# Chunked attention with a gated MLP on one core: the transfers of V to the two partition halves alternate, and the first three units load V in eight pieces

## The chip, the cores and the metric

The program runs on one core of one Trainium2 chip. The metric is the time of one execution on the device in microseconds, lower is better. The inputs are laid out on the host before the launch (q and k transposed, V rolled and cut into chunks of 32 rows), and that is not part of the time.

## The reference

Everything is float32. The attention part has batch B = 4, heads H = 8, length S = 768 and head size D = 64. Each chunk of 32 queries sees 8 memory keys and a window of 16 keys to the left, its own 32, and 8 to the right.

```python
for c in range(nc):                              # 24 chunks of 32 queries
    k_full = concatenate([mem_k, k[l_start:r_end]])
    v_full = concatenate([mem_v, v[l_start:r_end]])
    scores = scale * q_c @ k_full.T
    a = exp(scores - max(scores)); a = a / (sum(a) + 1e-9)
    out[:, :, chunk] = a @ v_full
x = out as (4, 768, 512)
h = relu(x @ w_in)                               # 512 -> 1024
u, v = h[..., :512], h[..., 512:]
v_n = (v - mean(v)) / sqrt(var(v) + 1e-6)
v_s = w_spatial @ v_n + b_spatial                # mixes the 768 tokens
return (u * v_s) @ w_out                         # 512 -> 512
```

## The kernel before

**Units.** The attention is cut into 24 units of 128 tokens (4 chunks, all 8 heads); six units make one batch. Each unit i goes through the same steps: ACT copies its keys into `kmain` (L375), PE makes the scores `sx<-kmain,q` (L388, "S" below), VectorE subtracts the maximum (`mx` L441, `p` L445), ACT takes the exponential (L450), VectorE sums (L455 to L458), PE transposes the weights (`pt`, L472), ACT copies them to `pT` (L475), PE multiplies them by V (`sx<-vmain,pT`, L388, "A" below), VectorE scales the result (`xs`, L424), PE transposes it (`xt`, L487), and the result is split into a high part (`x`, ACT L492) and a low part (`x`, VectorE L496). `p` and `pT` have one buffer each.

**MLP.** Each product by `w_in` is three matmuls per 128 columns: high by high (L525), low by high (L526) and high by low (L527). `ffn_v` makes one group per unit (128x512), `ffn_u` four per three units (128x384). The weights come as float64 in eight transfers `big<-in_moe_w_in_dram`; ACT (L825, L830), VectorE (L834, L835) and GpSimd (L840) turn each into float32, and L854 and L858 split it into `win_h` and `win_l`. The normalized v half and the u half go out to DRAM (`vn_far`, `u_far`) and come back for the second part, in which the spatial product and `w_out` are done with Strassen-like sums (L647 to L686).

**V in SBUF.** `vmain` holds three units. Partitions 0 to 63 serve the even heads (r = 0), 64 to 127 the odd heads (r = 1). In each half the first 32 rows are the chunk's own, 8 rows hold the memory values (written by the spread copies, L370), and 24 rows come from the next chunk. So a unit's V takes four transfers, of 32, 24, 32 and 24 partitions with runs of 1 KB, 0.46 MB together. `load_v` issues them, and `v_keys` names what the product A of a unit has to wait for.

**What sets the order.** Nothing is written in execution order. `Plan` gets every operation with an engine, an estimated duration and a rank, simulates the engines and one DMA pipe (0.30 MB per us), and emits each engine's instructions in the order of that simulation. A transfer counts there with `slow` (for its size) times `drag`. Nearly all transfers are issued by SP, in the order of the plan; those of one `line` (q, k, V, weights) keep the order of the code, and the stores find places between them. Each engine executes strictly in its emitted order. SP's transfers share eight semaphores in turn (`DMAHW0` to `DMAHW7`), so a transfer is issued only after the one eight before it has landed. Beside that `held_by` paces them by megabytes, with a wide window for the first 9 MB.

```python
    load_qk(0, (0,)); load_qk(0, (1,))
    # four w_in_part(c, 1, ...), the columns of ffn_v
    load_v(0); load_qk(1); w_in_part(0, 0, ...)
    load_v(1); w_in_part(1, 0, ...)
    load_v(2); w_in_part(2, 0, ...); w_in_part(3, 0, ...)
    # from unit 1 on, attend(i) is followed by load_v(i + 2)
```

## Time and profile before

| what | value |
|---|---|
| three runs | 380.58, 380.65, 384.18 us; median 380.65 us |
| the profiled execution | 378.39 us, of which the span of the trace is 376.2 us |
| PE busy | 355.6 us, 95% |
| VectorE, ACT, GpSimd busy | 275.0 us (73%), 188.8 us (50%), 139.8 us (37%) |
| mean granted PE clock | 0.991 |
| DMA | 65.12 MB, mean 173 GB/s |

The share of each engine is an average over a start of some 40 us, a long middle and an end. The profiled execution lies 2.26 us below the median of the three runs, so a difference is best worked out against the profiled execution and then carried over to the median.

### The profile page before, as it was taken

Reading aid. Unit: us, or ns where it says so; the run is one execution under the profiler, and the core shown is the slowest. Engines: PE = TensorE matmul, PEld = TensorE weight load, DVE = VectorE, ACT = ScalarE, POOL = GpSimd, SP = SyncE. Lnnn points to the kernel's source line nnn. Section 1 sums busy time; section 2 is a strip of 40 time slices with the busy share of each in tenths; the row PEclk is TensorE's granted clock in tenths of the full one; section 3 lists DMA queues with packets and bytes.
Section 4 is the critical chain, followed back from the end, with each engine's and each line's share of the span. In section 5 each row is a group of like instructions: output and inputs, shape, how many; then the busy total and the mean of one; then the engine's idle time right before and its main releaser. Section 6 shows DMA issues by size and latency. Waiting matters only on the chain.

```text
span 376.2 us, 11734 instructions
## 1 busy us (share of the span) xinstructions
PE 355.6 (95%) x4964; PEld 327.8 (87%) x4964; DVE 275.0 (73%) x470; ACT 188.8 (50%) x336; POOL 139.8 (37%) x143
## 2 busy tenths in 40 slices
PE   1569899999999999999999999999999999999996
PEld 1357698898988988989889899999999999999996
DVE  3887875757767667775498589787858795896694
ACT  3757544554654456354473366327533742553371
POOL 5444652383484088510033195251026002203410
PEclk9969999999999999999999999999999999999999
DMA  8998888888786783865832649204720582140014
GB/s 230 290 233 228 186 250 232 230 234 250 218 237 192 251 232 92 264 212 181 233 142 92 216 142 319 101 0 167 250 89 0 170 257 80 61 144 8 2 44 167
DMA packets 47368, 65.12 MB, mean 173 GB/s; under 512 B 4434, under 2 KB 38866, under 8 KB 47316
## 3 DMA queue, kind: packets, MB, share of 16 engines
q1 hardware_dynamic: 46900, 64.25, 56.4%
q8 instruction: 39, 0.64, 0.7%
q10 hardware_dynamic: 416, 0.13, 0.1%
q14 instruction: 13, 0.11, 0.1%
HBM read 45.49 MB, written 18.87 MB: 171 GB/s over the span
## 4 chain that ended last, share of the span: by engine, by line
PE 91%; DVE 4%; ACT 2%; DMA 1%; issue 1%; SPq 0%; ACTq 0%; DVEq 0%
PE y L686 22%; PE f L686 17%; PE f L525 13%; PE f L526 12%; PE f L527 12%; PE sx L388 10%; PE xt L487 3%; PE pt L472 3%; DMA k<-in_k_dram 1%; DVE st L835 1%; DVE st L834 1%; DVE mx L441 1%; DVE p L445 0%; PE y L680 0%; PE f L680 0%
## 5 line engine op out<-in xcount | busy, mean ns | idle before, releaser
L742 POOL TENSOR_TENSOR ug<-st,ug 128x384 f32<-128x384 f32 x24 | 33.1, 1392 | 97.7 <-DVE st L734 97.7
L686 PE MATMUL y<-wsp,op 128*128 128x384 f32 x288 | 52.6, 336 | 0.0
L686 PEld LDWEIGHTS y<-wsp,op 128*128 128x128 f32 x288 | 50.1, 188 | 0.0
L525 PE MATMUL f<-x,win_h 128*128 128x384 f32 x128 | 46.3, 362 | 0.0
L527 PE MATMUL f<-x,win_h 128*128 128x384 f32 x128 | 43.1, 337 | 0.0
L526 PE MATMUL f<-x,win_l 128*128 128x384 f32 x128 | 43.0, 336 | 0.0
L525 PE MATMUL f<-win_h,x 128*128 128x512 f32 x96 | 41.7, 435 | 0.0
L686 PE MATMUL f<-wsp,op 128*128 128x384 f32 x216 | 40.1, 336 | 0.0
L526 PE MATMUL f<-win_h,x 128*128 128x512 f32 x96 | 38.6, 402 | 1.5 <-DVE x L496 1.5
L664 DVE TENSOR_TENSOR op<-sm,op 128x768 fp32r<-128x768 f32 x32 | 33.4, 1050 | 7.2 <-ACT op L661 6.6
L527 PE MATMUL f<-win_l,x 128*128 128x512 f32 x96 | 38.4, 400 | 0.0
L686 PEld LDWEIGHTS f<-wsp,op 128*128 128x128 f32 x216 | 37.6, 188 | 0.0
L686 PE MATMUL y<-wout,op 128*128 128x256 f32 x288 | 35.7, 280 | 0.0
L424 DVE TENSOR_TENSOR xs<-sx,rec 128x512 f32<-128x512 f32 x24 | 16.5, 689 | 25.8 <-PE sx L388 25.6
L686 PEld LDWEIGHTS y<-wout,op 128*128 128x128 f32 x288 | 34.8, 188 | 0.1
L661 ACT CAST op<-sm 128x768 fp32r<-128x768 f32 x32 | 26.3, 838 | 15.5 <-DVE sm L647 7.7
L571 POOL TENSOR_TENSOR rstd<-ve,mhalf 128x1 f32<-128x1 f32 x24 | 14.6, 610 | 52.2 <-DVE ve L567 51.8
L388 PEld LDWEIGHTS sx<-kmain,q 64*32 64x32 f32 x1536 | 17.5, 110 | 17.1 <-POOL vmain L370 9.5
L388 PE MATMUL sx<-kmain,q 64*32 64x64 f32 x1536 | 21.5, 235 | 10.6 <-ACT kmain L375 8.4
L596 ACT ACTIVATE uo<-f 128x384 f32<-128x384 f32 x32 | 15.6, 491 | 24.5 <-PE f L527 23.0
L370 POOL COPY vmain<-memv 8x1024 f32<-8x1024 f32 x22 | 23.5, 1075 | 10.2 <-PE sx L388 8.5
L686 PE MATMUL f<-wout,op 128*128 128x256 f32 x216 | 27.1, 280 | 0.0
(92 smaller groups left out, 732.8 us busy)
## 6 DMA issues: line engine op xcount, KB each, us to landing
vmain<-in_v_dram SPq DMA_DIRECT2D x48, 128.0 KB
vn_far<-st SPq DMA_DIRECT2D x24, 256.0 KB
u_far<-uo SPq DMA_DIRECT2D x32, 192.0 KB
vr<-vn_far SPq DMA_DIRECT2D x8, 768.0 KB
ug<-u_far SPq DMA_DIRECT2D x16, 384.0 KB
q<-in_q_dram SPq DMA_DIRECT2D x11, 512.0 KB
out_dram<-ot SPq DMA_DIRECT2D x36, 128.0 KB
vmain<-in_v_dram SPq DMA_DIRECT2D x47, 96.0 KB
```

The costliest lines, as they stand in the source:

```text
L370: {"DVE": nc.vector, "POOL": nc.gpsimd}[eng].tensor_copy(to, of)
L388: nc.tensor.matmul(o, w_, m, start=True, stop=True, skip_group_check=True)
L424: nc.vector.tensor_tensor(xs.rearrange("p t r d -> p r t d"), t_["sx", i][:, :, 1], rec.rearrange("p t r -> p r t").unsqueeze(3).broadcast ...
L525: nc.tensor.matmul(o, lh, rh, start=(j == 0), stop=False)
L526: nc.tensor.matmul(o, ll, rh, start=False, stop=False)
L527: nc.tensor.matmul(o, lh, rl, start=False, stop=(j == len(pairs) - 1))
L571: nc.gpsimd.tensor_tensor(a, t_["ve", i], mhalf, op=ALU.pow)
L596: op("ACT", act(HT), lambda: nc.scalar.activation(alloc("uo", i, [P, HT], F32), t_["f", n], AF.Relu), r=[("f", n)], w=[("uo", i)], rank=rank)
L661: nc.scalar.copy(half(0), of())
L664: nc.vector.tensor_tensor(half(1), of(), half(0).bitcast(F32), op=ALU.subtract)
L686: nc.tensor.matmul(o, x, y, start=first and m == 1 and not (seed and bank != "x"), stop=m == 3 * chunks, skip_group_check=True)
L742: nc.gpsimd.tensor_tensor(g, t_[st(x)], g, op=ALU.mult)
```

## The change

The transfers of one unit are issued in another order: first the 32-row transfer of each half, then the 24-row one of each half. For units 0, 1 and 2 each of them is cut in two along t (the pairs of heads), so that such a unit comes in eight transfers of 64 KB or 48 KB. The argument `second`, which no call used, goes. The plan's `drag` for V falls from 1.5 to 1.2, so the plan believes that V arrives sooner.

```diff
-    def load_v(i, seq=True, second="SP"):
+    def load_v(i, seq=True):
...
-        for r in range(2):
-            v4 = v_of(i).rearrange("p t c d -> p t (c d)")
...
-                load(dst, src_, w=[("vm", i, r, s)], rank=10.0 * i, slow=1.2, us=0.38, seq=seq, drag=1.5,
-                     eng=second if r else "SP")
-            part(v4[p0:p0 + CH], src(v, g0 * D, [[G * D, CH], [TS, T], [1, n * D]]), 0, CH)
-            o = v4[p0 + SLOT:p0 + D]
-            if g0 + 2 * (T - 1) * NC + n < G:
-                part(o, src(v, (g0 + 1) * D, [[G * D, nr], [TS, T], [1, n * D]]), 1, nr)
...
+        def part(r, dst, src_, s):
+            load(dst, src_, w=[("vm", i, r, s)], rank=10.0 * i, slow=1.2, us=0.38, seq=seq, drag=1.2)
+        v4 = v_of(i).rearrange("p t c d -> p t (c d)")
+        step = (T if i >= 3 else T // 2)
+        for t0 in range(0, T, step):
+            t1 = t0 + step
+            for r in range(2):
+                g0 = (b * H + r) * NC + c0
+                part(r, v4[r * D:r * D + CH, t0:t1], src(v, g0 * D + t0 * TS, [[G * D, CH], [TS, step], [1, n * D]]), t0)
+        for t0 in range(0, T, step):
+            t1 = t0 + step
+            for r in range(2):
+                g0 = (b * H + r) * NC + c0
+                o = v4[r * D + SLOT:r * D + D]
+                if g0 + 2 * (T - 1) * NC + n < G or t1 < T:
+                    part(r, o[:, t0:t1], src(v, (g0 + 1) * D + t0 * TS, [[G * D, nr], [TS, step], [1, n * D]]), T + t0)
...
     def v_keys(i):
-        return [("vm", i, r, s) for r in range(2) for s in range(4)] + \
+        return [("vm", i, r, s) for r in range(2) for s in range(2 * T + 2)] + \
```

The transfers of V are 110 instead of 98. Line numbers behind `load_v` are 7 higher in the changed kernel. Since the plan decides the order, the change also moves instructions that it does not name. Three places matter below.

On SP, at the start, behind the first four loads of `w_in`, before the change (`vmain` is V in SBUF, `big` the raw `w_in`):

```order
L257 DMA big<-in_moe_w_in_dram 128x1024 x4
L257 DMA vmain<-in_v_dram 32x4x256
L257 DMA vmain<-in_v_dram 24x4x256
L257 DMA vmain<-in_v_dram 32x4x256
L257 DMA vmain<-in_v_dram 24x4x256
L257 DMA q<-in_q_dram 128x4x256
L257 DMA k<-in_k_dram 128x4x288
L257 DMA big<-in_moe_w_in_dram 128x1024
```

and with the change:

```order
L257 DMA big<-in_moe_w_in_dram 128x1024 x4
L257 DMA vmain<-in_v_dram 32x2x256 x4
L257 DMA vmain<-in_v_dram 24x2x256 x4
L257 DMA q<-in_q_dram 128x4x256
L257 DMA k<-in_k_dram 128x4x288
L257 DMA big<-in_moe_w_in_dram 128x1024
```

The q and k of units 2 and 3 stand behind eight transfers instead of four.

On PE, at the start, around the first product by V (`sx<-vmain,pT`), before the change:

```order
L540 MATMUL f<-win_h 128x512 x4
L472 MATMUL pt<-ident,p 128x128 x4
L388 MATMUL sx<-vmain,pT 32x64 x32
L487 MATMUL xt<-ident,xs 128x128 x4
L388 MATMUL sx<-kmain_144,q 32x64 x32
```

and with the change:

```order
L547 MATMUL f<-win_h 128x512 x4
L395 MATMUL sx<-vmain,pT 32x64 x32
L479 MATMUL pt<-ident,p 128x128 x4
L494 MATMUL xt<-ident,xs 128x128 x4
L395 MATMUL sx<-kmain_144,q 32x64 x32
```

The product of unit 0 by V now stands ahead of the transpose of unit 1's weights.

On VectorE, in the third MLP group, around the low part of unit 2 (`x<-xt,x`), before the change:

```order
L424 TENSOR_TENSOR xs<-sx,rec 128x2x4x64
L441 TENSOR_REDUCE mx<-sx 128x8
L575 TENSOR_SCALAR st<-st,mvar,rstd 128x512
L834 TENSOR_SCALAR st<-st 128x512
L835 SCALAR_TENSOR_TENSOR st<-big,st 128x512
L445 TENSOR_TENSOR p<-sx,mx 128x2x4x64
L496 TENSOR_TENSOR x<-xt,x 128x4x128
L563 BN_STATS stats<-st 128x6
```

and with the change:

```order
L431 TENSOR_TENSOR xs<-sx,rec 128x2x4x64
L448 TENSOR_REDUCE mx<-sx 128x8
L452 TENSOR_TENSOR p<-sx,mx 128x2x4x64
L503 TENSOR_TENSOR x<-xt,x 128x4x128
L582 TENSOR_SCALAR st<-st,mvar,rstd 128x512
L841 TENSOR_SCALAR st<-st 128x512
L842 SCALAR_TENSOR_TENSOR st<-big,st 128x512
L570 BN_STATS stats<-st 128x6
```

The normalization of unit 0 and the two steps on `w_in` now stand behind the low part of unit 2 instead of ahead of it.

## The prediction

> **What bounds the kernel now.** I read the page first, then the busy time by stretches, then PE's waits.

> ```profile
> span 376.2 us, 11734 instructions
> PE 355.6 (95%) x4964; PEld 327.8 (87%) x4964; DVE 275.0 (73%) x470; ACT 188.8 (50%) x336; POOL 139.8 (37%) x143
> ```

> PE leaves only 376.2 - 355.6 = 20.6 us idle. In the stretches the columns are the length, the busy time of PE, PEld, DVE, ACT and POOL with their counts, the granted PE clock, the DMA share and GB/s.

> ```profile
> 0.00:10.00 10.00, 1.17 (x64) 0.96 (x64) 3.75 (x8) 2.94 (x4) 6.10 (x13) 1.00 0.85 240
> 10.00:20.00 10.00, 6.31 (x140) 4.36 (x140) 9.00 (x15) 7.54 (x14) 4.38 (x4) 1.00 1.10 288
> 20.00:25.00 5.00, 2.19 (x69) 1.79 (x70) 4.58 (x10) 3.66 (x7) 1.61 (x1) 0.74 0.96 227
> 25.00:30.00 5.00, 5.00 (x48) 3.68 (x47) 3.07 (x7) 1.58 (x4) 1.29 (x1) 0.58 0.97 249
> 30.00:35.00 5.00, 4.49 (x187) 3.55 (x172) 4.18 (x9) 4.21 (x8) 3.15 (x3) 1.00 0.96 244
> 35.00:40.00 5.00, 3.49 (x17) 2.43 (x17) 4.93 (x8) 3.98 (x7) 2.72 (x4) 1.00 0.66 199
> ...
> 42.00:200.00 158.00, 157.97 (x3244) 139.04 (x3230) 110.17 (x227) 82.62 (x145) 71.14 (x81) 1.00 0.71 211
> 200.00:364.00 164.00, 164.00 (x1135) 161.78 (x1134) 126.83 (x175) 77.65 (x141) 47.76 (x37) 1.00 0.36 122
> 364.00:376.20 12.20, 8.97 (x76) 8.72 (x75) 6.61 (x13) 3.98 (x10) 0.00 (x0) 1.00 0.38 130
> ```

> From 42 to 364 us PE is busy without a gap, so nothing can be won there, only lost. The last 12.2 us have 3.2 idle and hold no V. All the rest, 8.83 + 3.69 + 2.81 + 0 + 0.51 + 1.51 = 17.35 us, lies before 40 us. Who ends these waits:

> ```profile
> PE sx L388 <- ACT kmain L375: 8.4, 2, 7.1
> PE f L540 <- ACT win_h L854: 2.9, 1, 2.9
> PE xt L487 <- DVE xs L424: 1.9, 1, 1.9
> PE f L526 <- DVE x L496: 1.5, 1, 1.5
> ```

> These 14.7 of the 17.35 us wait for ACT and VectorE, none for a transfer of V. The 7.1 and the 2.9 come ahead of the first use of V. So a faster V by itself buys nothing; what can change the time is the order that the plan makes of it, and a V, q or k that comes too late.

> **Part 1: the transfers.** V moves slowly. Between 41 and 44 us SP's traffic is V alone; from 48 to 50 us it is mostly q and k, in runs of about the same size.

> ```profile
> 41.00:44.00 3.00, 3.00 (x75) 2.33 (x74) 2.83 (x6) 0.57 (x2) 2.76 (x3) 1.00 1.04 162
> 48.00:50.00 2.00, 2.00 (x73) 1.66 (x72) 1.22 (x2) 0.63 (x1) 1.94 (x3) 1.00 1.07 378
> ```

> A unit (0.46 MB) takes 2.8 us at 162 GB/s and would take 1.2 us at 378. Taking turns could win anything from 0 to 1.6 us of DMA time per unit; I take the lower quarter, 0.4, since each transfer still goes to one half only. On the sum it is worth 0 either way: DMA ended no wait of PE above, and its share is 0.71 in the long middle.

> [...] The rows here show the slow V, but nothing on alternation.

> **Part 2: eight pieces on SP.** Twelve more issues, and a transfer waits for the landing of the one eight before it.

> ```profile
> 10.75 0.39 SPq L257 DMA_DIRECT2D k<-in_k_dram  x1
> 14.43 0.35 SPq L257 DMA_DIRECT2D big<-in_moe_w_in_dram  x1
> 14.82 2.33 SPq L257 DMA_DIRECT2D vmain<-in_v_dram  x4
> 17.37 0.97 SPq L257 DMA_DIRECT2D big<-in_moe_w_in_dram  x1
> 19.10 5.04 SPq L257 DMA_DIRECT2D vmain<-in_v_dram  x4
> 24.79 0.82 SPq L257 DMA_DIRECT2D big<-in_moe_w_in_dram  x2
> ```

> One issue costs at most 2.33 / 4 = 0.58 us, waits included, the twelve 7.0 us of SP, spread over a start in which SP also waits (5.04 us for four). Now the eighth piece of unit 0 waits for the fourth `w_in` load. That one had landed by 14.82, when the transfer eight behind it went out. So the eighth piece leaves at about 14.8, q at 15.3, k at 15.9 instead of 10.75. That looks bad but is covered: unit 0's seven pieces keep the pipe full until then. From 14.8 on at most 0.46 MB of V at 162 GB/s (2.8 us) and 0.52 + 0.59 MB of q and k (128x4x256 and 128x4x288 floats) at 378 (2.9 us) are ahead, so k lands at 14.8 + 2.8 + 2.9 = 20.5, and V of unit 0 at 17.6. Who waits for them:

> ```profile
> 17.62 1.11 PE L472 MATMUL pt<-ident,p 128*128 128x128 f32 x4 [0.17 <-ACT p L450]
> 18.66 0.98 PE L388 MATMUL sx<-vmain,pT 64*32 64x64 f32 x64
> 19.76 0.59 ACT L475 COPY pT<-pt 128x512 f32<-128x512 f32 x1 [1.69 <-PE sx L388]
> 20.78 0.68 DVE L424 TENSOR_TENSOR xs<-sx,rec 128x512 f32<-128x512 f32 x1
> 22.21 0.59 ACT L492 CAST x<-xt 128x512 fp32r<-128x512 f32 x1 [1.34 <-PE xt L487]
> 22.69 0.73 ACT L375 COPY kmain<-k 128x640 f32<-128x640 f32 x1
> ```

> k is needed at 22.7, 2.2 us after my 20.5. V is needed by the A product, which the change puts ahead of pt: A at 17.7 to 18.7, pt to 19.8, the pT copy at 19.9 instead of 19.76. xs cannot start before 20.78 anyway, for VectorE is 4.58 of 5 us busy there, and ACT has 1.34 us to spare ahead of x. So V may land 1.34 - 0.14 = 1.2 us later, at 18.8, without cost. The first MLP group starts where it did. Term: 0, with bounds -0.2 and +0.5 us.

> **Part 3: the order on VectorE.** This is the one wait that the change takes up: PE's 1.51 us that end at 39.33. The first rows are of the chain, the last of ACT in order of time.

> ```profile
> 35.47 0.45 DVE st L575
> 35.92 1.45 DVE st L834
> 37.39 0.69 DVE st L835
> 38.08 0.60 DVE p L445
> 38.68 0.61 DVE x L496
> 39.33 0.50 PE f L526
> ...
> 36.70 0.57 ACT L492 CAST x<-xt 128x512 fp32r<-128x512 f32 x1
> ```

> The low part of unit 2 (`x`, L496) has its input from ACT at 36.70 + 0.57 = 37.27, but VectorE first normalizes unit 0 and works on `w_in` for 37.39 + 0.69 - 35.47 = 2.6 us. With the change p stands directly behind mx (35.47 to 36.1), and x follows when ACT is done: 37.3 + 0.7 = 38.0, so L526 starts near 38.06 instead of 39.33. **Gain 1.27 us**, at most the 1.51 that PE waited, and at least 0.7 if ACT, whose order changes there too (a step on `w_in` moves ahead of the cast to `win_h`), is late by one operation of 0.59. What is late next: the displaced L575, L834 and L835 now end near 39.7 instead of 38.1. L575 releases the store of unit 0, off the path. L834 and L835 feed GpSimd and `win_l` of a later column block, whose first reader is a `ffn_u` group; the plan fills that place with five blocks of other groups. Cost 0, or the 1.6 us of the displacement if that cover is gone.

> **Part 4: the rest of the order.** PE's 841 rows hold the same work, but up to unit 13 attention and MLP are interleaved otherwise. The tightest step is A, xs, xt: counting the matmuls between A and xt of a unit at 0.24 us (128x512) and 0.18 (128x384), the least before is 1.23 us, with the change 1.08 (unit 4) and twice 1.24 (units 5 and 8). xs takes 0.69, and with the semaphores some 0.9, so each fits, unless VectorE is on another 0.7 us operation when A ends; then the three places lose 0.5 + 0.35 + 0.35 = 1.2 us. I take 0.2, near the lower end, since in the whole of 42 to 200 us comparable places left PE idle for 0.03 us.

> **The sum** against the profiled execution: 0 + 0 - 1.27 + 0.2 = -1.1 us, 378.39 becomes 377.3 (span 375.1). That execution stands 2.26 us below the median of the runs shown, so the median goes from 380.65 to **379.5**, which I round to 379.4. This is a change of 0.3%, and about 1% is what a measurement of this kernel can tell from no change.

> **Rivals.**
> - *Given back.* The gain of part 3 is lost where the order is tighter (1.2 us of part 4) or where `win_l` comes late (1.6): the median stays at 380.7, at worst 382.1. For it: VectorE is busy 4.18 and 4.93 of 5 us from 30 to 40 us. Against: no gap of PE after 42 us.
> - *The clock.* PE was granted 0.74 and 0.58 from 20 to 30 us, and a matmul took twice as long:

> ```profile
> 26.23 0.43 PE f L525
> 41.20 0.24 PE f L525
> ```

>   If the changed start keeps PE busier, twelve matmuls gain 0.19 each, 2.3 us: 377.1 with part 3. Against: A moves ahead of pt, so the idle stretch before xt at 21.5 remains.
> - *Slower: the eighth piece.* Between 14.43 and 24.79, when the seventh `w_in` load goes out, SP issued ten transfers (1 + 4 + 1 + 4) with eight in flight, 8 x 1.04 = 8.3 us from issue to landing each. If the last piece of unit 0 takes that long, V lands at 23.1, and everything behind A (pt, pT, x, the keys of unit 2) moves with it. It decides from 18.8; the price is 4.3 us, and with part 3 the median is 383.7, or 385.0 when the gain of part 3 goes too. Against: those 8.3 us are the backlog of up to eight large transfers, and here only 0.46 MB is ahead.
> - *The change does not do what it says:* V stays at 162 GB/s because each transfer still goes to one half. Part 3 comes from the plan's lower `drag`, not from the chip, so the time is the forecast's, whose sum takes nothing from a faster V. I count it in the forecast.

> **How the numbers follow.** Forecast, with either rate of V, 0.58; given back 0.20; the clock 0.08; the eighth piece 0.08; an unforeseen start 0.06. The forecast's own sum runs from -1.51 - 0.2 = -1.7 to -0.7 + 0.5 + 0.2 = 0.0 us, a median of 378.9 to 380.7. To leave out no more than 2 in 10 the range reaches from the clock (377.1) nearly to the eighth piece: 376.8 to 382.8. Faster by over 1% (below 376.84) needs the clock and more of the start: 0.09. Slower by over 1% (above 384.46) needs the eighth piece with all else lost: 0.08. Within 1%: 0.83.

> **What would show it.** Right: PE's wait for `x` (L503 with its new number) falls from 1.5 us to 0.3 or less, the row of waits for `kmain`, `win_h` and `xs` stays within 0.3 us, PE is busy without a gap from 42 us on, and the first MLP matmul starts at 24.6 within 0.5. Part 1 is seen in GB/s where V is alone on SP: 162 now, some 185 by my 0.4 us. Part 2 is wrong if A of unit 0 waits for a transfer beyond 18.8 us or the keys of unit 2 come after 22.7. Part 4 is wrong if PE waits for `xs` or for the next `win_l` between 42 and 110 us. The whole is wrong if the granted clock of 20 to 30 us changes, or if a wait for k appears on ACT that holds up its evacuations of the MLP groups.

## The result and the profile after

The change takes **383.72 us** in the median of 20 runs (379.89 to 386.86), the kernel before 380.74 us (379.1 to 386.05) beside it. The ratio is 1.0074, 95% interval 1.005 to 1.0097: slower by 0.7%, where 379.4 us (0.3% faster) had been forecast. Run again in a second series it was 385.03 us against 382.23, ratio 1.0091 (1.0054 to 1.0128). Ratios here use the runs within 1.5% of the shortest of their kernel, which matters where a kernel's runs spread widely. The profile shown is of that second series, a run of 386.48 us; the one that came with the first (386.86 us) stops at the same places. Both stand near the top of their spread, and before's profile (378.39 us) is shorter than any of the 20 runs beside it. So the two profiles lie 8 us apart where the medians lie 3 us apart: the profiles show where time goes, not how much of it a median run loses.

The page of the change:

```profile
span 384.5 us, 11754 instructions
PE 357.6 (93%) x4964; PEld 329.4 (86%) x4964; DVE 275.0 (72%) x470; ACT 188.6 (49%) x336; POOL 139.7 (36%) x143
```

Against before's 376.2 and 355.6 the span is 8.3 us longer: PE is busy 2.0 us more for the same 4964 matmuls, and idle 26.9 instead of 20.6 us. PE's waits (total, times, longest):

```profile
PE sx L395 <- ACT kmain L382: 8.2, 2, 6.9
PE sx L395 <- issue: 6.3, 3, 4.3
PE f L547 <- ACT win_h L861: 2.9, 1, 2.9
PE xt L494 <- DVE xs L431: 2.6, 2, 2.3
...
PE f L533 <- issue: 1.6, 1, 1.6
```

The wait for `x` (1.5) is gone, as forecast, and those for `kmain` and `win_h` stand. New are 6.3 + 1.6 us of "issue": PE waits, and the profile names nothing that it waits for. Before had 0.3 us of it. The longest piece, in the rows of PE in order of time, first before, then the change:

```profile
32.69 0.78 PE L388 MATMUL sx<-vmain,pT 64*32 64x64 f32 x54
33.75 0.33 PE L388 MATMUL sx<-vmain,pT 64*32 64x64 f32 x10 [0.28 <-issue]
34.01 0.50 PE L525 MATMUL f<-win_h,x 128*128 128x512 f32 x1
```

```profile
32.29 0.74 PE L395 MATMUL sx<-vmain,pT 64*32 64x64 f32 x51
37.31 0.46 PE L395 MATMUL sx<-vmain,pT 64*32 64x64 f32 x13 [4.28 <-issue]
37.70 0.79 PE L532 MATMUL f<-win_h,x 128*128 128x512 f32 x1
38.30 0.63 PE L533 MATMUL f<-win_h,x 128*128 128x512 f32 x1
38.72 0.63 PE L534 MATMUL f<-win_l,x 128*128 128x512 f32 x1
```

PE stops **inside** one product, A of unit 2, after 51 of its 64 matmuls. None of the 13 matmuls behind the stop has a wait of its own: the product's last semaphore wait was passed at 32.62 us. And when it goes on, it goes at half pace, 0.42 us from one matmul to the next where it is 0.23 us from 42.4 us on; the windows (length, PE, PEld, DVE, ACT, POOL, granted clock, DMA share, GB/s) show the clock:

```profile
30.00:35.00 5.00, 2.80 (x132) 2.11 (x123) 3.35 (x7) 3.80 (x7) 3.21 (x4) 1.00 1.03 242
35.00:40.00 5.00, 2.69 (x18) 2.04 (x19) 1.98 (x3) 1.72 (x3) 1.27 (x1) 0.54 0.84 227
40.00:45.00 5.00, 5.00 (x22) 3.88 (x20) 2.79 (x6) 2.80 (x5) 0.57 (x1) 0.78 0.29 85
```

That second stretch at half clock is the 2.0 us of additional busy time. The 6.3 us of idle time are made up so: this stop 4.28 - 0.28 = 4.0; two more of its kind, 0.87 at 72 us and 1.62 at 97 us; 1.18 at 55 us of another kind (below); 0.45 more ahead of the first xt; less the 1.51 of `x`. That is 6.6, some 0.3 too much.

### The profile page after: what moved, and what is told of

It reads as the page before. It is cut to its first block, busy times and chain, and to the rows that moved or that the text cites. A ratio compares the mean times of both kernels' runs of the same rounds, so it can differ in the third digit from the quotient of the medians.

```text
span 384.8 us, 11754 instructions
## 1 busy us (share of the span) xinstructions
PE 357.6 (93%) x4964; PEld 328.7 (85%) x4964; DVE 276.3 (72%) x470; ACT 188.1 (49%) x336; POOL 139.6 (36%) x143
## 4 chain that ended last, share of the span: by engine, by line
PE 89%; DVE 5%; issue 3%; DMA 1%; ACT 1%; SPq 0%; DVEq 0%; ACTq 0%
PE y L693 22%; PE f L693 16%; PE f L532 12%; PE f L533 11%; PE f L534 11%; PE sx L395 10%; PE xt L494 3%; PE pt L479 2%; DMA k<-in_k_dram 1%; DVE st L841 1%; DVE st L842 1%; DVE xs L431 1%; DVE p L452 0%; PE y L687 0%; PE f L687 0%
## 5 line engine op out<-in xcount | busy, mean ns | idle before, releaser
L532 PE MATMUL f<-win_h,x 128*128 128x512 f32 x96 | 41.8, 435 | 0.0
L671 DVE TENSOR_TENSOR op<-sm,op 128x768 fp32r<-128x768 f32 x32 | 32.6, 1023 | 7.8 <-ACT op L668 7.2
L395 PE MATMUL sx<-vmain,pT 64*32 64x64 f32 x1536 | 23.7, 227 | 6.7 <-issue 6.7
L395 PEld LDWEIGHTS sx<-vmain,pT 64*32 64x32 f32 x1536 | 19.6, 107 | 9.8 <-issue 8.8
```

The source lines that it names most:

```text
L395: nc.tensor.matmul(o, w_, m, start=True, stop=True, skip_group_check=True)
L532: nc.tensor.matmul(o, lh, rh, start=(j == 0), stop=False)
L671: nc.vector.tensor_tensor(half(1), of(), half(0).bitcast(F32), op=ALU.subtract)
```

## What PE waited for

The trace's DMA records list a queue "instruction" of 39 packets of 16384 bytes. PE has 10,008 instructions in before's trace, some 256 for each packet, so I take these packets to be PE's program. The third packet started at 31.17 us in before and at 34.37 us in the change. The place of a stop can be counted: with matmuls, weight loads and semaphore instructions, the stop at 33 us comes ahead of PE's instruction 962, that of 0.87 us ahead of 2242 and that of 1.62 us ahead of 3266. The distances are 1280 = 5 x 256 and 2304 = 9 x 256. So the first theory was that **PE had run out of instructions**, because its next packet came late.

The third packet never started before PE had passed instruction 705, and 962 - 256 is 706. From this I estimate that PE asks for a packet some 256 instructions ahead (later packets started when PE was up to 41 instructions short of that distance).

*Theory 1*: the third packet is late because of the transfers in flight when it is asked for. *Theory 2*: the plan's new order, through tighter steps from 45 us on, makes the change slow. *Theory 3*, a reason for the first: the eight pieces of the third unit fill all eight places in flight with 0.46 MB, the DMA runs dry at 26 to 28 us, and the last two `w_in` loads come later and in a bunch with what follows. SP's rows of the change and the DMA in that window (length, clock, share, GB/s), and then the window in before:

```profile
21.94 0.36 SPq L257 DMA_DIRECT2D big<-in_moe_w_in_dram  x1
22.34 4.43 SPq L257 DMA_DIRECT2D vmain<-in_v_dram  x8
26.87 1.03 SPq L257 DMA_DIRECT2D big<-in_moe_w_in_dram  x2
27.99 1.72 SPq L257 DMA_DIRECT2D vmain<-in_v_dram  x4
```

```profile
26.00:28.00 2.00, 0.50 0.35 81
```

```profile
26.00:28.00 2.00, 0.50 1.07 215
```

The two `w_in` loads left 2 us later than in before (24.79).

## The experiments

**The change again, and its parts.** In all of these but the one with more matmuls the other engines' order is that of before or of the change to the last row; only what is named differs. "Turns" means that the transfers alternate between the two halves, "pieces" that those of the first three units are cut in two.

> The changed kernel itself, with a profile of a shorter run to set beside before's 378.4 us. Theory 1 (PE's instruction fetch arrives late behind bunched transfers): the product A of unit 2 again stops in the middle for some 5 us at 33 to 38 us with no releaser named, and the 16384-byte packet of PE's instruction queue that was served at 35.4 us in the first profile is served late again. Theory 2 (the tighter order): the idle time of PE lies in waits for xs and p between 45 and 120 us, some 2 to 3 us, and the stop at 33 us is an accident of one run. About 383 us by either; if the stop is an accident of some runs, 379 to 380.

Measured: shown above; the stop recurs at the same instruction. The profiled run is again a long one, so a shorter run of the change has not been traced.

`load_v` was rewritten so that what the plan sees (the change's transfers or before's, and its `drag`) and what SP then issues in those places (turns or not, cut or not) are set apart:

```diff
+    PLAN_NEW, REAL_NEW, DRAG, SPLIT = True, False, 1.2, False
...
+        slots = v_parts(i, PLAN_NEW, PLAN_NEW and i < 3)
+        reals = v_parts(i, REAL_NEW, SPLIT and i < 3)
+        for j, (_, s_) in enumerate(slots):
+            mine = reals[-(-j * nr_ // ns):-(-(j + 1) * nr_ // ns)]   # issued at place j
```

*The new order with before's transfers* (the four values as above):

> The new order of all engines' work, but V in the four whole transfers a unit of before, without turns. Theory 1 and 3 (the eight pieces starve and then bunch the transfers, and PE's instructions come late): the stop at 33 us is gone, and with part 3's gain the time is 379.4 to 380.7, ratio 0.997 to 1.000. Theory 2 (the order itself): as slow as the change, ratio 1.005 to 1.01, with the waits for xs and p in 45 to 120 us still there.

Measured: 381.62 us, ratio **0.9982** (0.9936 to 1.0028). PE passes through A of unit 2 without a stop, and the third packet starts at 31.32 us. So the order alone does not make the change slow, and theory 2 falls. It does give its gain back, though, at one place that I had not priced. Rows of VectorE and then of PE:

```profile
48.53 1.30 DVE L486 TENSOR_TENSOR den<-den,eps 128x8 f32<-128x8 f32 x1
49.87 0.20 DVE L488 RECIPROCAL rec<-den 128x8 f32<-128x8 f32 x1
50.16 0.11 DVE L469 MEMSET sx<- 32x64 f32 x1
50.30 0.69 DVE L471 TENSOR_REDUCE mx<-sx 128x8 f32<-128x512 f32 x1
```

```profile
51.10 0.96 PE L418 MATMUL sx<-vmain,pT 64*32 64x64 f32 x64 [1.17 <-issue]
```

A starts 0.11 us after `mx` has ended (50.99): both use the one `sx` buffer, and PE's semaphore instruction ahead of A, one of whose two waits is for VectorE, ends at 51.04. The 1.17 us return in the change (1.18 us ahead of its instruction 1512, 550 behind 962 and so no multiple of 256), so by the count of theory 1 this is no want of instructions.

*Before's order with the change's transfers:*

```diff
-    PLAN_NEW, REAL_NEW, DRAG, SPLIT = True, False, 1.2, False
+    PLAN_NEW, REAL_NEW, DRAG, SPLIT = False, True, 1.5, True
```

> The order of before on every engine but SP, with the change's transfers of V (turns for all units, eight pieces for the first three). Theory 1 and 3: slower, ratio 1.005 to 1.015, with a stop of PE without a releaser near 33 to 38 us or with the two w_in loads behind V2 landing 1.5 us or more later than in before. Theory 2: no slower than before, ratio 0.997 to 1.002.

Measured: 383.87 us in the median of all twelve runs, 378.15 to 388.26, against 382.23 for before, or 0.4% more. The ratio by the rule above (0.9967, 0.9919 to 1.0015) rests on about half of these runs, so it cannot judge this kernel. The time alone thus decides neither for theory 1 (1.005 to 1.015) nor for theory 2; the trace of a run of 384.57 us does: PE stops for 5.19 us after 51 of 64, the packet starts at 34.20, and the DMA share of 26 to 28 us is 0.34. With the order of before the pieces and turns bring the stop.

*The new order with turns, nothing cut* (`True, True, 1.2, False`):

> The new order and turns in every unit, but no cut: four whole transfers a unit. Theory 1 and 3: as e1, 379.4 to 380.7, and any difference to e1 is the turns alone (my prediction held them worth 0 on the sum). Theory 2: as slow as the change, 1.005 to 1.01.

Measured: 380.32 us, ratio 0.9981 (0.9948 to 1.0014), the same as without turns. Its trace, of a run near that median, has the packet at 32.71 and a stop of 2.13 us.

**Is it the place in the program?** One of the four matmuls `f<-win_h` at 15 us (`keep_warm` in the code; nothing reads their result) was replaced by 32 small ones, ahead of everything that matters here.

```diff
-            for _ in range(passes):
+            for _ in range(passes - 1):
                 nc.tensor.matmul(o, win_h[:, c, DH:DH + P], win_h[:, c, DH:], start=True, stop=True)
+            for _ in range(32):
+                nc.tensor.matmul(o[0:CH, 0:D], win_h[0:D, c, DH:DH + CH].bitcast(F32), ..., start=True, stop=True)
```

> The changed kernel with one of the four warming matmuls at 15 us replaced by 32 small ones, so that PE has 31 matmuls more in its program ahead of the place where it stopped. Theory 1 (PE ran out of fetched instructions): the stop is tied to a place in PE's program, not in the work, so it again follows the 471st matmul or so, which is now some 31 matmuls earlier in the work: after about 20 of the 64 matmuls of A of unit 2 instead of 51, some 3 to 5 us long. Rival (a wait for data of A, that the trace does not show): the stop stays after 51 of the 64. The time is that of the change, 382 to 387 us, by both.

Measured: 390.66 us in one run, above the 382 to 387 expected. Each small matmul counts as two in the trace, so PE has 63 more ahead, not 31, and they took 6.9 us, which is why all comes later. The stop moved with the program:

```profile
35.24 0.81 PE L395 MATMUL sx<-kmain,q 64*32 64x64 f32 x58 [0.22 <-DVE xs L431]
38.73 0.31 PE L395 MATMUL sx<-kmain,q 64*32 64x64 f32 x6 [2.68 <-issue]
```

It again comes ahead of instruction 962, which now lies in S of unit 3, 61 matmuls earlier in the work, and A of unit 2 runs through. A wait for data of A is excluded.

**Is it the traffic?** SP holds the first transfer of V of unit 3 until the last `w_in` load has landed, once in the change and once in before:

```diff
+    def calm():
+        quiet[:] = [flight[-1][0]]      # transfer() waits for it
...
+            if i == 3 and r == s == 0:
+                dst = lambda d=dst: (calm(), d)[1]
             load(dst, src_, w=[("vm", i, r, s)], ...
```

> The change, but the first transfer of V of unit 3 waits on SP until the last w_in load has landed, so that at 30 us only the last two w_in loads are in flight. V3 is used at 37 us at the earliest, q of group 2 and k behind it later. Theory 1 (the instruction packet is late because of the transfers that are in flight when it is asked for): the packet is served before 33 us instead of 34.4 to 35.4, PE's stop of 4 to 5 us shrinks below 2 us, and the time falls to 379.5 to 382, ratio 0.995 to 1.003. Rival (the packet is late for a reason on PE's side, or the stop has another cause): the stop stays, ratio 1.005 to 1.012; a new wait for V3 or q at 37 to 42 us may come on top.

Measured: 382.73 us, ratio 1.0054 (1.0023 to 1.0086), against 1.0091 without the hold. The time misses theory 1's 379.5 to 382 and lies in the rival's band. But the packet starts at 31.81 us, and the big stop shrinks, both as theory 1 had it:

```profile
32.63 0.74 PE L404 MATMUL sx<-vmain,pT 64*32 64x64 f32 x51
34.13 0.34 PE L404 MATMUL sx<-vmain,pT 64*32 64x64 f32 x13 [0.76 <-issue]
```

The DMA ran dry at 26 to 28 us here too (share 0.35), so the hole by itself does not delay the packet; with V of unit 3 out of the way after 30 us it comes earlier. How much the DMA moves is not the measure: from 30 to 35 us its share was 0.96 in before, with the packet in time, and 1.03 in the change. The rest of the excess (span 380.7 us against before's 376.2) is 2.3 us of idle and 2.2 of busy time. The stops at instructions 3266 and 2242 are still 1.59 and 0.43 us, A waits 0.85 us at 50 us, and behind the stop at 3266 the granted clock is 0.50 from 94.1 to 97.4 us.

> The kernel before with the same hold: V3's first transfer waits until the last w_in load has landed. Theory 1: before's profile had the packet in time (31.2 us), so its shorter runs gain nothing, but its longer runs (383 to 386 us) get fewer: median 379 to 381, ratio 0.99 to 1.0. Rival: no difference, or slower by a late V3, q or k (A of unit 3 is at 41.8 us): ratio 1.0 to 1.005.

Measured: 379.25 us, ratio **0.9948** (0.9922 to 0.9974), and no run above 380.9. That is the time that theory 1 expected; the trace does not show the reason, for its packet starts at 31.64 us, no earlier than in the traces of before (30.74 to 31.46), which are all of runs below 380 us.

**Which pieces?** The change with the third unit whole again (`SPLIT and i < 2`, plan as in the change):

> The change with V of the third unit in four whole transfers instead of eight pieces (units 0 and 1 stay cut, turns stay). Theory 3 (the eight pieces of the third unit leave only 0.46 MB in flight at 26 to 28 us, DMA share 0.35, and push the last two w_in loads behind): the DMA share of 26 to 28 us is 0.8 or more, the last w_in load goes out before 26.5 us, the packet comes at 31 to 33 us, and the ratio is 0.997 to 1.003. Rival (the pieces of the first two units are enough): the stop stays, ratio 1.005 to 1.01.

Measured: 380.09 us, ratio **0.9993** (0.9963 to 1.0023). The window of this kernel:

```profile
26.00:28.00 2.00, 0.50 1.02 231
```

The last two `w_in` loads go out from 24.18 us, the packet starts at 30.79, a little ahead of the 31 to 33 expected, and PE's stop after 52 of 64 is 0.19 us. Against the change (1.0091) only the third unit's transfers differ, and the two intervals lie apart: the pieces of the first two units cost nothing that can be measured; those of the third carry the loss, some 1%.

**Turns alone, and the hold with others.** First turns with before's order (`False, True, 1.5, False`), then before with the hold again, the hold with turns, and the hold with turns and the new order.

> The order of before with turns alone: nothing cut, no hold. By the prediction's part 1 and theory 3 it is the time of before, ratio 0.996 to 1.002; if turns alone also make the instruction packet late (it came 1.5 us later with the new order and turns than with the new order without), 1.002 to 1.008 and PE's stop after 474 matmuls is above 1 us.

Measured: 381.48 us, ratio 1.0003 (0.9968 to 1.0037). Both branches of the expectation came: the time of before, and in the traced run (382.9 us) the packet at 32.92 and a stop of 2.11.

> The kernel before with the hold ahead of V3, once more, to see its advantage again on this chip and beside the next three. If the hold removes PE's stops of the longer runs, the ratio is again 0.992 to 0.998 and the spread 378 to 381 us; if the first result was chance, 0.997 to 1.002.

Measured: 380.0 us, ratio 0.9983 (0.9954 to 1.0012), with one run of 1184.53 us. The advantage of the hold is not certain in this series; together the two say 0.2 to 0.5%.

> The order of before, turns in every unit, nothing cut, with the hold ahead of V3: against the kernel before with the hold only the turns differ. If turns are worth nothing on the sum, 378.5 to 380.5 us as that kernel; if a faster V (252 GB/s where it was alone with turns, 155 before) frees the instruction packets further, 377 to 378.5.

Measured: 379.83 us, ratio 0.9962 (0.993 to 0.9994), with one run of 1184.49 us; turns are worth nothing on the sum here either.

> The new order of all engines and turns in every unit, nothing cut, with the hold ahead of V3. The order alone was worth nothing (1.5 us won at the wait for x, 1.2 and 0.8 us lost at 50 and 66 us), so 378.5 to 380.5 us, ratio 0.992 to 0.999, the same as the order of before with the hold. If the new order had a gain that the packet's lottery hid, 377 to 378.

Measured: 380.27 us, ratio 0.9981 (0.9944 to 1.0017).

**More traced runs of two kernels**, for the link between packet, stop and time:

> The order of before with the change's transfers, a second look. Its runs spread from 378.2 to 388.3 us. If the late instruction packet makes the difference, the run's time less its PE stops that follow the 471st to 474th matmul and the later ones without a releaser (and the half clock behind them) is the same in every run, about 376 to 378 us: a run of 379 shows the packet before 32 us and a stop under 1 us, a run of 384 the packet after 34 us and a stop of 4 to 5 us. If not, a short run shows the stop too.

> As the look before this one; a third point for the time against the packet. A run near 379 us has it before 32 us, a run near 384 us after 34 us.

> The kernel before, a second look. Its runs spread from 378.1 to 386.5 us. By the packet theory a run above 381 us has a PE stop without a releaser of 1 us or more, at the 471st to 474th matmul or at a later multiple of 256 instructions from there; a run below 380 has none above 0.5 us.

> The kernel before, a third look: above 381 us with a stop of PE of 1 us or more without a releaser, below 380 us with none above 0.5 us.

Measured: 383.89, 382.24, 379.50 and 378.94 us. None of these is a run of the pieces near 379 us or one of before above 381, so what was expected of those is not tested. Of the bounds that were, several failed: before at 379.50 and 378.94 us has stops of 1.37 and 0.76, above the 0.5 set, and the pieces at 383.89 us have the packet at 33.2, ahead of the 34 set, and a stop of 2.82 where 4 to 5 had been set. The size of one stop is not read from the time of a run to a microsecond; between kernels the picture is plain, by the start of the third packet:

```
kernel (run, us)                     PE at instr. 705   third packet   stop at 962
before (378.94)                           29.43            30.74          0.76
change, third unit whole (379.68)         29.95            30.79          0.19
turns + hold (378.62)                     29.91            31.15          0.52
before (378.39)                           30.27            31.17          0.28
new order alone (379.50)                  30.42            31.32          none
before + hold (378.56)                    30.22            31.33          0.21
before (379.50)                           29.66            31.46          1.37
before + hold (379.57)                    30.30            31.64          0.45
new order, turns + hold (381.05)          30.42            31.78          0.49
change + hold (382.67)                    30.16            31.81          0.76
new order, turns (380.54)                 29.87            32.71          2.13
turns alone (382.90)                      30.23            32.92          2.11
pieces alone (383.89)                     29.97            33.23          2.82
pieces alone (382.24)                     29.73            33.72          3.83
pieces alone (384.57)                     29.08            34.20          5.19
change (386.48)                           29.82            34.37          4.28
change (386.86)                           29.98            35.36          5.12
```

From 31.8 us on the stop grows with the start of the packet; the run of 384.57 us stands out because PE came there 0.7 us earlier and so waited longer. The five traces of the table with the third unit in pieces and no hold have the packet at 33.2 us or later, all others before 33. All of them with pieces were also with turns, and turns without pieces have it at 32.7 and 32.9; pieces without turns were not run.

## Why the prediction was wrong

**Part 1, the transfers: right on the sum, open on the rate.** V alone moved at 162 GB/s in before's profile, and I forecast 185. A window of the change:

```profile
46.00:48.00 2.00, 1.00 0.82 187
```

That is nearly the forecast, though a q had been issued behind V at 45.91 us. It does not show that turns make V faster. The rate of V alone varies from run to run of before: in its two later traces, with nothing but V issued from 37.9 to 43.5 us, it is 194 and 205 GB/s from 41 to 44 us. Turns alone have 199 from 42.5 to 45.5 us, inside that spread. On the sum it buys nothing, as forecast: 0.9981 with turns and 0.9982 without, 1.0003 for turns alone.

**Part 2, the eight pieces: the step that failed.** I traced them to the operations that need V, q and k, and there they were harmless, even early: q leaves SP at 14.30 us (15.3 forecast), A of unit 0 starts at 17.10 without a wait, and the first MLP matmul is at 24.31 (24.6 forecast). But I followed unit 0 only, and counted the twelve additional issues as SP's time. Their real price is bytes: the third unit's pieces hold all eight places in flight, where whole transfers leave room for the `w_in` loads. The pipe drains (DMA share 0.35 from 26 to 28 us against 1.07), 1 MB of weights moves 2 us back (26.87 us against 24.79), V of unit 3 comes on top of it, and a transfer that stands in no list of the program, the packet that I take for PE's own code, is 3 us later (34.37 us against 31.17). The term of 0 (-0.2 to +0.5) was 4.0 us of stop and 2.0 us of half clock in the profiled run, a long one. Over all runs it was some 3 to 4 us: 1.0091 with the third unit in pieces against 0.9993 with it whole is 1.0% of 381 us.

**Part 3, `x`: right.** The wait is gone; that part of the forecast was worth 1.27 and the row gives 1.51 us.

**Part 4, tighter steps: mis-sized.** I put 0.2 us, up to 1.2, on A, xs, xt. What it cost was `mx` ahead of A, 1.17 us at 50 us, a distance that I had not counted. The new order alone thus comes out at 0.9982, not measurably faster.

**The rivals.** "Given back" is what the order did, and its 1.2 us was met by chance, since the place was `mx` and not A, xs, xt. "The eighth piece" had the time right by chance, 383.7 us, and its mechanism is refuted: no transfer of unit 0 was late. "The clock" from 20 to 30 us hardly changed (0.68 and 0.64 against 0.74 and 0.58); it fell in a place that I had not named, behind the stop. That a busier PE would be granted more was my assumption, which no run here shows. Nor does that early clock set the time: from 20 to 30 us before was granted 0.66 in its run of 378.39 us and 1.00 in that of 379.50. Of my tests, the one for gaps of PE behind 42 us did answer (1.18, 0.87 and 1.62 us); but all of them would have missed the main loss, which lies at 33 us and belongs to no tile.

**What stays open.** Which of the sixteen DMA engines carries a packet, and how it stands among data there, the records do not tell; that traffic delays it rests on the hold and on the third unit's pieces. Why turns came with a packet at 32.7 and 32.9 in two traces, without a longer median, is not settled, nor what decides whether the later stops, at 2242 and 3266, come: before has them in some of its traces too (0.43 and 1.08 us).

## What to carry to other kernels

With a fixed number of transfers in flight, cutting a transfer in two halves the bytes in flight: the third unit's eight pieces were 0.46 MB. Look at the DMA share just behind the pieces (0.35 here, against 1.07 in before), and at the large load that queues behind them. Where a profile charges a wait in the middle of a product to "issue", count instructions: here distances of 5 x 256 and 9 x 256 pointed to the packets of 16384 bytes, and the hold of one unit of V shortened the stop from 4.28 to 0.76 us in the traced runs. Holding one unit of V back until the last weight load had landed gave 0.9948 and 0.9983 in two series, 0.9962 with turns and 0.9981 with turns and the new order. It is the one step here that beats the kernel before, if by no more than 0.5%. It is not safe to take over as it stands: two of the 60 runs of kernels with the hold took 1184 us, and none of some 200 others did.
